# Grouped-query decode attention with a gated MLP: stretches of the TensorE program become loops, each head's closing work moves to the end of its group, and seven in place of five output slices go by 512-column matmuls

## The chip, the cores and the metric

The kernel runs on one core of a Trainium2 chip. The metric is device time in microseconds of that core, as a median of runs. All inputs lie in the chip's memory at the start, and the result is written there.

## The reference

Two tokens (B = 2) are decoded against a cache of 32,768 positions. Eight key/value heads serve 32 query heads, four queries a head, 128 elements each; everything is bf16.

```python
xn = _layernorm(x)
s  = _A_ref(xn, k_cache, v_cache, wq, wo)        # attention
g  = _silu(_B_ref(xn, w1, w2, w3, w4))           # MLP; with S = 1 its shifted halves are zero, so w1, w2 drop out
return x + s * g
...
q = (xn @ wq) per head;  scores = q.k * Dh**-0.5;  p = softmax(scores);  o = p.v;  s = o @ wo
h2 = gelu(layernorm(xn) @ w3) @ w4;  _B_ref = xn + h2
```

The two caches are 2 x 8 x 32,768 x 128 bf16 each, 134 MB; with `wq` (4 MB), `wo` (4 MB), `w3` and `w4` (1.8 MB each) 280.5 MB are read once.

## The kernel before, in words

**Groups.** A group is one (token, key/value head): 16 in all (`NG`). For each, K is one 8 MB DMA into two of the three slots of `kbuf`, V one 8 MB DMA into `vbuf`, which holds one group. All large DMAs are issued by SP, in one order: wq, w3, w4, K0, V0, K1, V1, and so on, then `wo` in six parts (`wo_parts`). K of group m waits on `pe.sem`, which TensorE raises when the first half of group m-1 is nearly scored (L702); V of group m waits on `ac.sem`, raised when ScalarE sees the values' product of group m-1 done (L495). The last group's K and V, and `wo`, come in smaller pieces.

**One group.** Counting groups from 0, a group runs thus. K's 128 rows a partition are two halves (`NPART`) of eight tiles (`NR`). VectorE transposes the 16 tiles (L589) into four buffers `T` (`T_BUFS`); TensorE takes them in pairs (`t_vt`) and multiplies each by `z`, the group's queries spread into a selection pattern, four 512-column matmuls a tile (L698), the first half into PSUM bank `sc[0]`, the second into `sc[1]`. VectorE waits for a tile's four matmuls before it overwrites that buffer (`used`). Then come maximum (`peak`, L568), a matmul that spreads it (`S`, L710), `shift`, Exp on ScalarE (L491), VectorE's transposes of the probabilities (L608), 64 matmuls with V in two halves (L722), and a matmul for the sums (L729). ScalarE copies the product `o` to `ob` (L496).

**A head's closing work** turns `ob` into a column of `oX`: `head_oT` on TensorE (four fp32 matmuls, L660), `head_on` on VectorE (sum, reciprocal and two products: L543 to L552, giving `on`), `head_xp` on TensorE (one matmul, L666), `head_out` on VectorE (L559, L565), a copy on GpSimd (L513). For group m this runs inside group m+1: `head_oT` between the two halves of the scores, `head_on` after tile 3 of the second half, `head_xp` after TensorE's tile 4 of the second half, `head_out` after the last transpose. So in group 0 it works on zeroed data. The last group's runs in `pe_output`.

**Ahead of the groups** stand layernorms, q (L403, 32 matmuls in four column blocks of the array, two transposes L408), `w3` (L424), gelu, `w4` (L439, 14 matmuls), sigmoid. V0 overwrites w3 and w4, so its issue waits for `w4`'s last matmul (`e_h2`, L454).

**Behind the groups** `pe_output` multiplies by `wo`. Slices k = 0 to 3 (part 0) come from `oX_w`, which a wide matmul (L740) and VectorE (`own_part`) make. A slice k < KC goes as four 512-column matmuls into `qrb` (L760); after the last of them ScalarE copies `qrb` to `wsum` (L646), and four fp32 matmuls with `comb` (L750) add it into `pro`. A slice k >= KC goes as 16 matmuls of 128 columns straight into `pro` (L768). KC is 5. VectorE then multiplies by the gate and adds x (L647, L648), and two small DMAs write the output.

TensorE's own program is one straight stretch ahead of the groups, one loop `pe_groups` over 16 groups, whose body is both halves unrolled, and `pe_output`.

Of the kernel before, what the change touches and what calls it, by code (L numbers as in the profile page):

```python
# [21 lines left out]
T_BUFS = 4  # L22
# [44 lines left out]
class LateQueue(Queue):  # L67
# [13 lines left out]

    def place(self):
        for emit, need, inc in self.kept:
            for s, v in need[:-1]:
# [34 lines left out]
def kernel(  # L119
# [37 lines left out]
    KC = 5  # L157
# [72 lines left out]
    sc = [bank(f"sc{i}") for i in range(NPART)]  # L230
# [49 lines left out]
    t_vt, t_vg, t_tv = (sem(f"t_{n}") for n in ("vt", "vg", "tv"))  # L280
# [26 lines left out]
    with tc.tile_critical(sync_engine=mybir.EngineType.Pool, no_gpsimd_drain=True):  # L307
# [20 lines left out]
        po.op(lambda e: e.memset(ob[:, :], 0.0), inc=(t_ob, 1))  # L328
# [5 lines left out]
        ve.op(lambda e: e.memset(S[:, 0:NPART * rep], 1.0), inc=(t_tv, 1))  # L334
# [55 lines left out]

        treg = qrb[:, :].bitcast(BF16)
# [6 lines left out]
        HH = Hq // NPART  # L398
        for i in range(NPART):
            for k in range(DK):  # L400
                for n in range(NQ):
                    last = k == DK - 1 and n == NQ - 1
                    e = pe.op(lambda t, i=i, k=k, n=n: t.matmul(  # L403
                        sc[i][32 * n:32 * n + B, :], lhsT=xT[:, k, :],
                        rhs=wq3[:, k, :].rearrange("p (h n y) -> p h n y", n=NQ, y=32)[:, i * HH:(i + 1) * HH, n, :],
                        start=(k == 0), stop=(k == DK - 1), tile_position=(0, 32 * n)),
                        e_xT, e_s00, inc=last)
            e = ve.op(lambda v, i=i: v.transpose(out=qT[:, i * 512:(i + 1) * 512], in_=sc[i][:, :]), e)  # L408
# [29 lines left out]
        for f in range(FK):  # L438
            e_h2 = pe.op(lambda t, f=f: t.matmul(  # L439
                h2[0:B, :], lhsT=h_bf[:, f * B:(f + 1) * B], rhs=w4v[:, f, :],  # L440
                start=(f == 0), stop=(f == FK - 1)), e, inc=f == FK - 1)
# [19 lines left out]
        for m in range(1, NG):  # L461
            base = m % 2
            if m < NG - 1:
                sp.op(lambda e, m=m, base=base: e.dma_start(
                    out=kbuf[:, base * SLOT:(base + NPART) * SLOT], in_=row_view(A_k_cache, *groups[m])),
                    (pe.sem, pe_0 + m), e_q, inc=(t_k[0], 16))
            else:
                for i, h in enumerate(order(m)):
                    sp.op(lambda e, m=m, h=h, base=base: e.dma_start(
                        out=kbuf[:, (base + h) * SLOT:(base + h + 1) * SLOT],  # L470
                        in_=row_view(A_k_cache, *groups[m])[:, h * SLOT:(h + 1) * SLOT]),
                        (pe.sem, pe_0 + m), inc=(t_k[i], 16))
            load_v(m, (ac.sem, ac_0 + m))
# [6 lines left out]

        def take(eng, s, n=1):
            eng.wait_ge(s, n).then_inc(s, -n)  # L482

# [46 lines left out]
        def used(par, n):  # L530
            return t_tv, par * N_T + n + 2 + (n >= NR) + (n >= NR + 5)
# [4 lines left out]
        def out_of(par, last=False):  # L536
            return t_tv, par * N_T + (2 if last else NR + 2)

        def turned(par, last=False):
            return t_tv, par * N_T + (3 if last else NR + 8)  # L540

        def head_on(c, par=0, last=False, behind=None):
            nc.vector.tensor_reduce(  # L543
                out=den[:, :], in_=S[:, 0:NPART * rep].rearrange("p (i h) -> p h i", h=rep),
                axis=AX.X, op=ALU.add).wait_op(*sum_of(par), "sem-ge").then_inc(*c.inc(t_d))
# [5 lines left out]
            nc.vector.wait_ge(*out_of(par, last))  # L551
            ins = nc.vector.tensor_mul(  # L552
                out=on[:, :, :], in0=oT[:, :].unsqueeze(1).broadcast_to([128, NQ, rep]), in1=recm[:, :, :]).wait_op(*e, "sem-ge")
            if last:
                ins.then_inc(t_vt, 1)
                behind()

        def head_out(c, par=0, last=False):
            nc.vector.tensor_mul(  # L559
                out=xm[:, :, :], in0=xp_b[:, :].rearrange("p (r h) -> p r h", r=NQ),  # L560
                in1=mask[:, :].unsqueeze(1).broadcast_to([128, NQ, rep])).wait_op(*turned(par, last), "sem-ge").then_inc(*c.inc(t_d))
# [64 lines left out]
        e_wd, e_ws, e_s = ((pe.sem, pe.n + NG + i) for i in (1, 2, 3))  # L626
# [12 lines left out]
        head_on(c, last=True, behind=own_part)  # L639
        e_oX[NG - 1] = head_out(c, last=True)  # L640
        for b in range(B):
            m, n = b * Hkv + KC, Hkv - KC - (b == B - 1)
            e_oXz = ve.op(lambda v, b=b, m=m, n=n: v.tensor_copy(
# [37 lines left out]
        pe.n, pe.seen = prologue.n + NG, prologue.seen  # L681
# [4 lines left out]
        for s, v in prologue._new((e_s00, e_const, e_hf, e_tf, e_s0)):  # L686
            nc.tensor.wait_ge(s, v)
        nc.br("pe_groups", engines=[PE])
        with nc.body("pe_groups", valid_engines=[PE]):
            for i in range(NPART):  # L690
                for r in range(NR):
                    if r % 2 == 0:
                        take(nc.tensor, t_vt, 2)
                    Tb = Ts[(i * NR + r) % T_BUFS][:, :].bitcast(BF16).rearrange("p (b c e) -> p b c e", b=NB, e=2)
                    zc = (NR - 1 - r) * rep
                    for nb in range(NB):
                        for w in range(2):
                            ins = nc.tensor.matmul(  # L698
                                sc[i][:, :], lhsT=z[:, nb, w, zc:zc + 128], rhs=Tb[:, nb, :, w],
                                start=(r == 0 and nb == 0 and w == 0),  # L700
                                stop=(r == NR - 1 and nb == NB - 1 and w == 1))
                            if i == 0 and r == NR - 1 and nb == 0 and w == 0:  # L702
# [30 lines left out]
            nc.regs_alu(turn, turn, 1, op=ALU.add)  # L733
            nc.br_lt(turn, NG, on_true="pe_groups", on_false="pe_output", engines=[PE])


        with nc.body("pe_output", valid_engines=[PE]):
            head_oT()
# [5 lines left out]
            take(nc.tensor, t_vt)  # L744
            head_xp()
            for i, (a, c, r0, r1) in enumerate(wo_parts):
                if i == 3:
# [5 lines left out]
                for k in range(a, c):  # L753
                    pe.wait(e_oXz if k >= KC else e_oX[(B - 1) * Hkv + k], (d_wo[i], n_wo[i]), *((e_wide,) if i == 0 else ()))
                    for r in range(r0, r1):
# [9 lines left out]
                        for n in range(NQ):  # L765
# [4 lines left out]
                                start=(i == 2 and r == r0 and n < OQ), stop=(last and n >= NQ - OQ), tile_position=(0, 32 * q)),  # L770
# [41 lines left out]
```

## Time and profile before

| | |
|---|---|
| median of 3 runs | 655.83 us (655.77 to 655.99) |
| span of the profiled execution, first to last instruction | 654.1 us |
| what lies around the span (median less span) | 1.7 us |
| bytes read | 280.50 MB |
| TensorE matmuls busy | 417.4 us (64%) |
| VectorE busy | 379.4 us (58%) |
| ScalarE busy | 39.7 us (6%) |
| GpSimd busy | 10.3 us (2%) |
| mean granted TensorE clock | 0.88 of full speed |

The timings and the profile are separate executions; the profile gives no total of its own beside the span, so the difference of 1.7 us is taken as the part outside it. Rows of the timeline read: start in us from the span's start, duration, engine, line, operation, tile written <- tiles read, count, and in brackets the idle time before it with what ended it. PE is TensorE, PEld its weight loads, DVE VectorE, ACT ScalarE, SP the queue that issues DMAs; a q behind an engine's name is its sequencer. Rows of the windows give, for a stretch of time, each engine's busy time, the granted TensorE clock, the DMA engines' mean busy share (over 1 where a packet is counted in the stretch in which it began) and GB/s.

### The profile page before, as it was taken

Reading aid. Unit: us, or ns where it says so; the run is one execution under the profiler, and the core shown is the slowest. Engines: PE = TensorE matmul, PEld = TensorE weight load, DVE = VectorE, ACT = ScalarE, POOL = GpSimd, SP = SyncE. Lnnn points to the kernel's source line nnn. Section 1 sums busy time; section 2 is a strip of 40 time slices with the busy share of each in tenths; the row PEclk is TensorE's granted clock in tenths of the full one; section 3 lists DMA queues with packets and bytes.
Section 4 is the critical chain, followed back from the end, with each engine's and each line's share of the span. In section 5 each row is a group of like instructions: output and inputs, shape, how many; then the busy total and the mean of one; then the engine's idle time right before and its main releaser. Section 6 shows DMA issues by size and latency. Waiting matters only on the chain. (4 is left out here: it accounts for less than half of the span.)

```text
span 654.1 us, 6304 instructions
## 1 busy us (share of the span) xinstructions
PE 417.4 (64%) x2476; PEld 159.3 (24%) x2476; DVE 379.4 (58%) x541; ACT 39.7 (6%) x90; POOL 10.3 (2%) x44
## 2 busy tenths in 40 slices
PE   1437386574858747485774838667484865748876
PEld 0013132221313212131321313222131322213223
DVE  5348193673919457291854729276481936738772
ACT  1200101000010100001000010100001010000101
POOL 1000000000000000000000000000000000000000
PEclk9859889697997969899796989969698896979999
DMA  8999999999999999998999999999999899999997
GB/s 367 435 449 449 442 393 449 445 449 401 437 445 449 433 405 449 445 449 389 449 445 449 417 421 445 449 445 393 449 445 449 389 449 445 449 425 411 437 429 292
DMA packets 6246, 280.54 MB, mean 429 GB/s; under 512 B 730, under 2 KB 868, under 8 KB 1380
## 3 DMA queue, kind: packets, MB, share of 16 engines
q1 hardware_dynamic: 6232, 280.50, 99.2%
q8 instruction: 2, 0.03, 0.0%
q10 hardware_dynamic: 12, 0.00, 0.0%
HBM read 280.50 MB, written 0.00 MB: 429 GB/s over the span
## 5 line engine op out<-in xcount | busy, mean ns | idle before, releaser
L589 DVE STREAM_TRANSPOSE T<-kbuf 128x1024 int32<-128x1024 int32 x256 | 294.8, 1211 | 180.1 <-DMA kbuf<-in_A_k_cache_dram 173.2
L698 PE MATMUL sc<-T,z 128*128 128x512 bf16 x1024 | 273.1, 420 | 179.5 <-PEq L482 179.2
L698 PEld LDWEIGHTS sc<-T,z 128*128 128x128 bf16 x1024 | 98.9, 104 | 346.6 <-issue 260.2
L722 PE MATMUL o<-vbuf,pt 128*16 128x512 bf16 x1024 | 70.4, 379 | 17.7 <-PEq L482 17.7
L491 ACT ACTIVATE ep<-sc,shift 128x512 bf16<-128x512 f32 x32 | 21.7, 683 | 502.7 <-ACTq L482 502.7
L722 PEld LDWEIGHTS o<-vbuf,pt 128*16 128x16 bf16 x1024 | 27.3, 88 | 64.9 <-issue 42.8
L568 DVE TENSOR_REDUCE mx<-sc 128x1 f32<-128x512 f32 x32 | 21.5, 672 | 30.1 <-PE sc L698 30.1
L673 PE MATMUL pro<-ob,comb 128*2 128x512 f32 x66 | 33.7, 592 | 0.0
L608 DVE STREAM_TRANSPOSE pt<-ep 128x512 bf16<-128x512 bf16 x32 | 22.6, 708 | 15.0 <-ACT ep L491 15.0
L710 PE MATMUL S<-mxr,same_h 128*128 128x448 f32 x32 | 15.8, 576 | 18.4 <-PEq L482 18.4
L660 PEld LDWEIGHTS oT<-sel_o,ob 128*128 128x128 f32 x136 | 17.7, 191 | 3.4 <-issue 0.7
L729 PE MATMUL S<-sm,ones_f 128*128 128x448 f32 x32 | 16.3, 592 | 0.0
L660 PE MATMUL oT<-sel_o,ob 128*128 128x4 f32 x136 | 16.2, 242 | 0.0
L600 DVE TENSOR_REDUCE shift<-S 128x1 f32<-128x64 f32 x16 | 3.6, 225 | 18.8 <-PE S L710 18.8
L496 ACT COPY ob<-o 128x512 f32<-128x512 f32 x16 | 9.4, 587 | 78.6 <-ACTq L482 78.6
L513 POOL COPY oX<-oXs 128x4 bf16 (+1 forms) x16 | 3.0, 188 | 518.7 <-POOLq L482 518.7
L710 PEld LDWEIGHTS S<-mxr,same_h 128*128 128x128 f32 x32 | 4.8, 188 | 26.1 <-issue 26.1
L572 DVE TENSOR_SCALAR mxr<-row_of,mx 128x32 f32<-128x32 f32 x32 | 7.7, 241 | 1.1
L673 PEld LDWEIGHTS pro<-ob,comb 128*2 128x2 f32 x66 | 4.2, 83 | 14.0 <-issue 10.4
L393 PE MATMUL qrb<-ident,xs_bf 34*128 34x34 bf16 x4 | 0.3, 198 | 11.1 <-DVE xs_bf L356 11.1
L729 PEld LDWEIGHTS S<-sm,ones_f 128*128 128x128 f32 x32 | 4.8, 188 | 6.9 <-issue 6.9
L506 POOL TENSOR_TENSOR z<-qr,quad 128x64 bf16<-128x64 bf16 x16 | 4.7, 294 | 103.2 <-POOLq L482 87.7
(100 smaller groups left out, 78.5 us busy)
## 6 DMA issues: line engine op xcount, KB each, us to landing
kbuf<-in_A_k_cache_dram SPq DMA_DIRECT2D x2, 4096.0 KB, 22.4
vbuf<-in_A_v_cache_dram SPq DMA_DIRECT2D x2, 4096.0 KB, 21.7
kbuf<-in_A_wq_dram SPq DMA_DIRECT2D x1, 4096.0 KB, 12.4
vbuf<-in_B_w_dram SPq DMA_DIRECT2D x2, 1792.0 KB, 18.0
kbuf<-in_A_wo_dram SPq DMA_DIRECT2D x1, 2048.0 KB, 30.8
kbuf<-in_A_wo_dram SPq DMA_DIRECT2D x3, 512.0 KB, 31.9
kbuf<-in_A_wo_dram SPq DMA_DIRECT2D x1, 384.0 KB
kbuf<-in_A_k_cache_dram SPq DMA_DIRECT2D x15, 27.5
```

Source lines behind the costliest of these rows:

```text
L491: nc.scalar.activation(out=ep[i][:, :], in_=sc[i][:, :], func=ACT.Exp, scale=inv_sqrt_dh, bias=shift[:, :], accum_out=rs[:, i:i + 1]).then ...
L496: nc.scalar.copy(out=ob[:, :], in_=o[:, :]).then_inc(t_ob, 1)
L568: ins = nc.vector.tensor_reduce(out=mx[:, i:i + 1], in_=sc[i][:, :], axis=AX.X, op=ALU.max)
L572: ins = nc.vector.tensor_scalar_mul(out=mxr[:, i, :], in0=row_of[:, :], scalar1=mx[:, i:i + 1]).wait_op(*c.at(t_d), "sem-ge")
L589: ins = nc.vector.transpose(out=Ts[n % T_BUFS][:, :].rearrange("p (b t k) -> p t b k", b=NB, t=RT), in_=kt[:, r * W:(r + 1) * W].rearrange ...
L608: ins = nc.vector.transpose(out=pt[h][:, :, :].rearrange("p r (t h) -> p t r h", h=rep), in_=ep[order(par).index(h)][:, :].rearrange("p (t ...
L660: ins = nc.tensor.matmul(oT[:, :], lhsT=ob[:, t * Dh:(t + 1) * Dh], rhs=sel_o[:, t, :], start=(t == 0), stop=(t == VT - 1))
L673: nc.tensor.matmul(pro[0:B, :], lhsT=comb[:, 0:B], rhs=ob[:, :], start=True, stop=True)
L698: ins = nc.tensor.matmul(sc[i][:, :], lhsT=z[:, nb, w, zc:zc + 128], rhs=Tb[:, nb, :, w], start=(r == 0 and nb == 0 and w == 0), stop=(r = ...
L710: nc.tensor.matmul(S[:, NPART * rep:NPART * (rep + SREP * 32)].rearrange("p (s c) -> p s c", s=SREP), lhsT=same_h[:, :], rhs=mxr[:, :, :]. ...
L722: ins = nc.tensor.matmul(o[32 * j:32 * j + VT * rep, :], lhsT=pt[h][:, r, a * VT * rep:(a + 1) * VT * rep], rhs=vt[:, u * VT:(u + 1) * VT, ...
L729: nc.tensor.matmul(S[:, 0:SSUM * NPART * rep].rearrange("p (s c) -> p s c", s=SSUM), lhsT=ones_f[:, :], rhs=sm[:, :, :].rearrange("p i h - ...
```

## The change

On TensorE:

- q is a loop of eight turns; each turn makes 512 columns by four matmuls into two PSUM rows (not four column blocks), alternating between the two banks, waits for `t_q`, and VectorE turns each chunk by four 32-partition transposes (32 in place of two).
- `w4`'s 14 matmuls are one, then a loop of six turns with two each, then one.
- The two halves of a group's scores are a loop of two turns over eight tiles; the bank is addressed by a register. `pe.sem` rises in both halves, and the counts of K's waits follow.
- `head_oT`, a wait for `on` (`t_on`) and `head_xp` stand at the end of the group's own body, ahead of the branch back; `pe_output` has no copies of them. TensorE takes `t_on` once before the first group too.
- The loop branches carry no branch hint; `pe_groups` had none before either.
- KC is 7, the comb matmuls stand ahead of the last part of `wo` (i == 5, not i == 3), and the single filler matmul `warm(1)` is gone.

On VectorE `head_on` stands after tile 2 of a group's first half, and `head_out` after tile 5. `oT` and `xp` are set to ones at the start. TensorE's program goes from 634 to 443 instructions.

```diff
+            if isinstance(emit, tuple):
+                nc, start, end, body = emit
...
+                with nc.Fori(start, end, engines=[PE]) as i:
+                    body(self.eng, i).then_inc(self.sem, 1)
...
-    KC = 5
+    KC = 7
...
-    sc = [bank(f"sc{i}") for i in range(NPART)]
+    sc2 = bank("sc", 512 * NPART)
+    sc = [sc2[:, 512 * i:512 * (i + 1)] for i in range(NPART)]
...
+        nc.vector.sem_inc(t_q, NPART)
...
+        def q_part(t, c):
+            take(t, t_q)
+            out_c = sc2[0:B, bass.ds((c & 1) * 512, 512)]
             for k in range(DK):
...
+                ins = t.matmul(
+                    out_c, lhsT=xT[:, k, :], rhs=wq3[:, k, bass.ds(c * 512, 512)],
+                    start=(k == 0), stop=(k == DK - 1))
+            return ins
+
+        pe.loop(nc, 0, NC, q_part, e_xT, e_s00)
+        for c in range(NC):
+            for n in range(NQ):
+                e = ve.op(lambda v, c=c, n=n: v.transpose(
...
+        def w4_part(t, j):
+            for i in range(W4N):
+                ins = t.matmul(
+                    h2[0:B, :], lhsT=h_bf[:, bass.ds(j * W4N * B + (1 + i) * B, B)],
+                    rhs=vbuf[:, bass.ds(j * W4N * D + W4O + (1 + i) * D, D)], start=False, stop=False)
+            return ins
...
+        pe.loop(nc, 0, (FK - 2) // W4N, w4_part)
...
-                    (pe.sem, pe_0 + m), e_q, inc=(t_k[0], 16))
+                    (pe.sem, pe_0 + NPART * (m - 1) + 1), e_q, inc=(t_k[0], 16))
...
+                        if i == 0 and r == 2:
+                            head_on(c, par)
+                        if i == 0 and r == 5:
+                            head_out(c, par)
                         if i == 1 and r == 3:
                             peak(c, 0)
-                            head_on(c, par)
-                head_out(c, par)
...
+        take(nc.tensor, t_on)
         nc.br("pe_groups", engines=[PE])
         with nc.body("pe_groups", valid_engines=[PE]):
-            for i in range(NPART):
+            with nc.Fori(0, NPART, engines=[PE]) as i:
...
-                                sc[i][:, :], lhsT=z[:, nb, w, zc:zc + 128], rhs=Tb[:, nb, :, w],
+                                sc2[:, bass.ds(i * 512, 512)], lhsT=z[:, nb, w, zc:zc + 128], rhs=Tb[:, nb, :, w],
...
-                    if i == 1 and r == 4:
-                        head_xp()
-                if i == 0:
-                    head_oT()
...
             nc.regs_alu(turn, turn, 1, op=ALU.add)
+            head_oT()
+            take(nc.tensor, t_on)
+            head_xp()
             nc.br_lt(turn, NG, on_true="pe_groups", on_false="pe_output", engines=[PE])
...
-            head_oT()
             pe.wait(e_sp, e_oX[NG - 2])
...
-            take(nc.tensor, t_vt)
-            head_xp()
             for i, (a, c, r0, r1) in enumerate(wo_parts):
-                if i == 3:
+                if i == 5:
...
-                    if i == 2:
-                        warm(1)
```

More of the change, by code (lines that the diff above doesn't have):

```diff
@@ L80, in op, with loop @@
         return None
+    def loop(self, nc, start, end, emit, *events):
+        self.kept.append(((nc, start, end, emit), self._new(events), True))
+        self.n += end - start
+        return (self.sem, self.n)
     def place(self):
         for emit, need, inc in self.kept:
+            if isinstance(emit, tuple):
+                nc, start, end, body = emit
+                for s, v in need:
+                    self.eng.wait_ge(s, v)
+                with nc.Fori(start, end, engines=[PE]) as i:
+                    body(self.eng, i).then_inc(self.sem, 1)
+                continue
             for s, v in need[:-1]:
@@ L278 @@
         n_wo[i] += 16
-    t_vt, t_vg, t_tv = (sem(f"t_{n}") for n in ("vt", "vg", "tv"))
+    t_vt, t_vg, t_tv, t_on, t_q = (sem(f"t_{n}") for n in ("vt", "vg", "tv", "on", "q"))
     t_z, t_ob, t_e, t_d, t_pv = (sem(f"t_{n}") for n in ("z", "ob", "e", "d", "pv"))
@@ L397 @@
             in_=treg[:, 0:64 * DK].rearrange("p (k s c) -> p s k c", k=DK, s=2)[:, :, :, 0:B]), e, (d_wq, 16))
-        HH = Hq // NPART
-        for i in range(NPART):
-            for k in range(DK):
[L401 to L408, printed above, removed]
+        HC = 512 // Dh
+        NC = Hq // HC
+        def q_part(t, c):
+            take(t, t_q)
+            out_c = sc2[0:B, bass.ds((c & 1) * 512, 512)]
+            for k in range(DK):
+                ins = t.matmul(
[6 more added lines that the diff above has]
+                e = ve.op(lambda v, c=c, n=n: v.transpose(
+                    out=qT[32 * n:32 * n + 32, c * 32 * HC:(c + 1) * 32 * HC],
+                    in_=sc[c % 2][0:32, :].rearrange("p (h n y) -> p n h y", n=NQ, y=32)[:, n, :, :]), (pe.sem, pe.n - NC + c + 1),
+                    inc=(t_q, 1) if n == NQ - 1 and c < NC - NPART else True)
         e_q = ve.op(lambda v: v.tensor_mul(
@@ L437 @@
         h2 = sc[1]
[L438 to L441, printed above, removed]
+        W4N = 2
+        def w4_part(t, j):
[4 more added lines that the diff above has]
+            return ins
+        assert (FK - 2) % W4N == 0
+        pe.op(lambda t: t.matmul(h2[0:B, :], lhsT=h_bf[:, 0:B], rhs=w4v[:, 0, :], start=True, stop=False), e, inc=False)
+        pe.loop(nc, 0, (FK - 2) // W4N, w4_part)
+        e_h2 = pe.op(lambda t: t.matmul(h2[0:B, :], lhsT=h_bf[:, (FK - 1) * B:FK * B], rhs=w4v[:, FK - 1, :], start=False, stop=True))
         e_tf = ve.op(lambda v: v.tensor_add(out=t_f[:, :], in0=xn[:, :], in1=h2[0:B, :]), e_h2)
@@ L638 @@
         e_wide = (ve.sem, ve.n + 2)
-        head_on(c, last=True, behind=own_part)
+        head_on(c, behind=own_part)
         e_oX[NG - 1] = head_out(c, last=True)
```

44 lines of the change are left out of this document (23 added, 21 removed).

## The prediction

> **What bounds the kernel now.** I read the page first, then the chain that ended last, then the DMA views, and only then the engines.
>
> ```profile
> span 654.1 us, 6304 instructions
> q1 hardware_dynamic: 6232, 280.50, 99.2%
> q8 instruction: 2, 0.03, 0.0%
> ```
>
> ```profile
> 617.12 33.53 DMA kbuf<-in_A_wo_dram
> ...
> 650.69 0.64 PE pro L768 x16
> ...
> 651.35 0.29 DVE sg L647
> ```
>
> The 16 DMA engines are busy 99.2% of the span with the 280.5 MB that must be read, and the chain ends in a DMA, 16 matmuls and two vector operations. So an edit to TensorE costs something only (1) if it makes SP issue a transfer so late that the DMA engines run dry, (2) if it lengthens the work behind the last landing, or (3) if it changes the DMA stream itself. For (1) I need the slack of each issue:
>
> ```profile
> DMA packets 5225, 249.40 MB, mean 433 GB/s; under 512 B 583, under 2 KB 601, under 8 KB 1097
> ...
> kbuf<-in_A_wq_dram SPq DMA_DIRECT2D x1, 4096.0 KB, 12.4
> ...
> DMA to landing us min/median/max: 26.0/26.7/33.0
> ...
> DMA to landing us min/median/max: 26.6/27.5/28.7
> ...
> DVE T L589 <- DMA kbuf<-in_A_k_cache_dram: 173.2, 17, 12.7
> ```
>
> At 433 GB/s (DMA view of 72.8 to 649 us) 8.39 MB take 19.4 us. The first DMA, which had no queue ahead, landed 12.4 us after its issue, 9.7 of them transfer: 2.7 us are fixed. A V (first of the two landing rows, L448) took at least 26.0, so it stood 26.0 - 19.4 - 2.7 = 3.9 us in the queue; a K (second, L464) 4.5 us; V0, the 33.0, 10.9 us. VectorE waits 173 us in all for K, some 10 us a group: compute inside a group is hidden as long as an issue moves by less than those slacks.
>
> **The change part by part.**
>
> *Ahead of the groups: covered.*
>
> ```profile
> 13.51 3.26 PE L403 MATMUL sc<-kbuf,xT 128*2 128x512 bf16 x32 [2.07 <-DVE xT L395]
> ...
> 16.83 0.72 DVE L408 STREAM_TRANSPOSE T<-sc 128x512 f32<-128x512 f32 x1 [0.68 <-PE sc L403]
> ...
> 24.23 3.18 PE L439 MATMUL sc<-vbuf,h_bf 128*2 128x512 bf16 x14 [2.38 <-DVE h_bf L436]
> 27.45 0.36 SPq L448 DMA_DIRECT2D vbuf<-in_A_v_cache_dram  x1
> ```
>
> q takes 13.51 to 17.55 with four column blocks side by side. One after the other, as L439 does the same shape (3.18 / 14 = 0.227 each), 32 take 7.3. A loop turn's waits, register operations and branch are shown by no row of q; bounds 0 (the sequencer ahead of the array) and 0.5 us; I take 0.3, near the branch row below, for eight turns 2.4. Four transposes of the last chunk: a quarter of 0.72 each at least, 0.22 with a start, 0.9 together. Sum 10.6 for 4.04: +6.5; `w4`'s six turns +0 to +1.5, taken +0.5. V0 is issued near 34.5, inside its slack of 10.9; even +9 for q is. If the cover were gone, the excess would be lost one for one. K0's compute waits for K0 in any case.
>
> *Inside a group: hidden, except in the last two.* I follow group 14, whose delay is handed to group 15, which the end follows.
>
> ```profile
> 583.11 5.75 DVE L589 STREAM_TRANSPOSE T<-kbuf 128x1024 int32<-128x1024 int32 x5 [10.97 <-DMA kbuf<-in_A_k_cache_dram]
> ...
> 585.62 9.32 PE L698 MATMUL sc<-T,z 128*128 128x512 bf16 x32 [8.66 <-PEq L482]
> ...
> 589.23 8.10 DVE L589 STREAM_TRANSPOSE T<-kbuf 128x1024 int32<-128x1024 int32 x7 [0.38 <-PE sc L698]
> ...
> 598.10 0.16 DVE L543 TENSOR_REDUCE den<-S 128x4 f32<-128x8 f32 x1
> ...
> 598.80 4.61 DVE L589 STREAM_TRANSPOSE T<-kbuf 128x1024 int32<-128x1024 int32 x4
> ...
> 603.34 0.13 DVE L559 TENSOR_TENSOR xm<-xp,mask 128x16 f32<-128x16 f32 x1
> 603.51 0.17 DVE L565 TENSOR_REDUCE oXs<-xm 128x4 bf16<-128x16 f32 x1
> ...
> 605.56 0.69 DVE L568 TENSOR_REDUCE mx<-sc 128x1 f32<-128x512 f32 x1 [1.88 <-PE sc L698]
> ...
> 612.08 9.13 DVE L589 STREAM_TRANSPOSE T<-kbuf 128x1024 int32<-128x1024 int32 x8 [1.76 <-DMA kbuf<-in_A_k_cache_dram]
> ...
> 614.12 1.02 PE L729 MATMUL S<-sm,ones_f 128*128 128x448 f32 x2
> ...
> 621.88 4.62 DVE L589 STREAM_TRANSPOSE T<-kbuf 128x1024 int32<-128x1024 int32 x4 [0.67 <-DMA kbuf<-in_A_k_cache_dram]
> ```
>
> ```profile
> 586.40:589.80 3.40, 3.40 (x9) 1.17 (x8) 3.02 (x4) 0.00 (x0) 0.00 (x0) 0.51 0.89 386
> ```
>
> ```profile
> L734 PEldq COMPARE_BRANCH x16: 76/208/228, 70.6 to 641.8; - x16
> ```
>
> TensorE now starts a group after two transposes. Changed, it stands at `t_on`, behind three transposes (583.11 + 3.45) and `head_on` (598.10 to 598.80, 0.70, and 0.1 for its end), with `head_xp`, the branch back (0.21 by the last row) and the loop's entry branch (another 0.21) behind that; with 0.3 for xp, waits and registers, 0.7. Scores start at 588.05, not 585.62: +2.4, a new wait, and what is queued behind it is the whole group's scores, for which VectorE's buffers wait. The clock is at 0.5 there (nine matmuls in 3.40 us), so tile 0's four matmuls end at 589.9 and tile 1's at 591.6. VectorE, back from `head_on`, has its buffers full at 588.4: it waits 1.5 for tile 0 and 0.55 for tile 1, against 0.38 now. `head_out` costs it 0.35 in the middle, where it was hidden in the 1.88 wait at 605.56. `head_on` only moves, `head_oT` falls into TensorE's idle time. Group 14's VectorE work, and so V's issue and the product with V, comes 2.05 - 0.38 + 0.35 = 2.0 us later, K's issue 2.4. Both are inside 3.9 and 4.5: no bubble, 2 us left.
>
> Group 15's K is there when group 14 ends, so this case differs: `on` is ready 2.33 us after the start of the sums' matmul (643.29 to 645.62 in the rows of the end), 614.12 + 2.0 + 2.33 = 618.45. Until then VectorE stands behind `head_on` after three tiles, where now it runs eight without a stop. TensorE starts at 619.15, tile 0 is through at 620.15 with a warm clock, VectorE's tiles 4 to 7 and `head_out` end at 625.0. The second half begins 3.1 later than 621.88, gets 0.70 back since `head_on` is no longer in it: everything behind it +2.4.
>
> *Behind the groups.*
>
> ```profile
> 643.29 1.02 PE L729 MATMUL S<-sm,ones_f 128*128 128x448 f32 x2
> ...
> 645.20 0.22 PE L740 MATMUL sc<-T,sel_w 128*128 128x128 bf16 x1
> ...
> 645.45 0.17 DVE L552 TENSOR_TENSOR on<-oT,recm 128x16 bf16<-128x16 f32 x1 [0.52 <-PE oT L660]
> ...
> 646.41 1.04 PE L760 MATMUL qrb<-kbuf,T 128*2 128x512 bf16 x16
> ...
> 647.29 0.39 PE L760 MATMUL qrb<-kbuf,oX 128*2 128x512 bf16 x4
> 647.74 0.59 ACT L646 COPY T<-qrb 128x512 f32<-128x512 f32 x1 [3.57 <-PE qrb L760]
> ...
> 649.07 0.81 PE L750 MATMUL pro<-T,comb 128*4 128x128 f32 x8
> ```
>
> The path is now compute to 647.3 and landings to 650.69. Changed: `on` 2.33 after L729's start; xp, the branch not taken (0.08) and the wide matmul's issue 0.4; wide matmul to part 0 as now (645.20 to 646.41) 1.2; part 0's 16 matmuls 0.9; twelve for k = 4, 5, 6 at 0.054 each (16 in 0.87), 0.65; their end 0.23; copy of `qrb` with its hand-over 0.65; comb 0.65 (under the modelled 0.81); the last four and their end 0.25. Together 7.26 from L729, which starts at 643.29 + 2.4: 652.95. Part 3's landing no longer ends last, the copy and comb do. Against 651.35 that is **+1.6**. The single operations are rows; the hand-overs may be off by 0.1 each, so +1.0 to +2.2.
>
> *The DMA stream.*
>
> ```profile
> q8 instruction: 1, 0.02, 5.2%
> ```
>
> ```profile
> 650.00:650.50 0.50, 0.36 (x14) 0.17 (x7) 0.00 (x0) 0.00 (x0) 0.00 (x0) 1.00 0.05 20
> ```
>
> Two packets of the whole run are instructions. One lies in 71.7 to 72.8 us (first row): 5.2% of 16 engines times 1.1 us is 0.92 us on one engine, which all the others do not lose; the view of 72.8 to 649 has none (its 5225 packets are all of q1). The other comes past 648.5. At the very end (second row) the mean share is 0.05, under one engine of 16: one engine still moves `wo` when the others are done, and TensorE waits for it. An engine that fetched 16 KB in group 0 is late by 0.92 in every later transfer. If the shorter program needs no such fetch while the groups stream, K14, K15 and `wo` all land up to 0.9 earlier: **-0.9** (bounds 0 and -0.92), on the compute chain as well, since it starts at K14. I take it, because at the time of the packet TensorE was in the last 140 of the 445 instructions that end its group loop, and the changed loop ends at its 328th.
>
> [...]
>
> [...]
>
> Sum against the profile: 654.1 + 1.6 - 0.9 = 654.8; the 1.7 us outside the span stay: **656.5** beside the median of 655.83.
>
> **The rivals.**
>
> [...]
>
> *The stream runs dry.* V's issue has 2 us left. Should the groups start later than I have it by more than 2 us (the cold stretch longer, the loop's addressing slow), each group loses the excess: 0.5 us too much is 15 x 0.5, 664. It decides from a V issue 3.9 us later than now. Against: every price in that path has a row.
>
> *Taken branches fetch.* Each turn's branch back could need its code again: a packet of 0.92 behind one of V's. Two a group would use up the 2 us left and lose about 1 us in each of 16 groups, and 14 turns of 0.92 ahead of V0 exceed its remaining 3.9 by 9: some 656 + 16 + 9 = 681. Against: the row has 15 taken branches over 305 instructions and one packet. [...]
>
> *The end stays hidden.* If my hand-overs at the end are too dear and the landings still end last, only the fetch counts: 655.83 - 0.9 = 654.9. For it: five slices' worth of matmuls shrink. Against: VectorE standing still behind `head_on` in group 15 is in the program's order.
>
> **How the numbers follow.** Forecast 0.48 (656.5, +-0.7), fetch stays 0.32, dry 0.05, branches fetch 0.03, hidden end 0.12. About 0.2%, 1.3 us, is what a measurement here can tell from no change: above 657.1 or below 654.5. Slower: two thirds of the second case, the third and fourth, and a tenth of the forecast, 0.35. Faster: a third of the last and a little of the forecast, 0.05. The range from 655.0 to 658.0 leaves out part of the last case, the dry and fetching ones and a sliver of the second.
>
> **What would show it.** V0 issued near 34.5; V's landing rows no lower than 23.9; scores starting 4.9 us, not 2.5, after a group's first transpose; VectorE idle 1.5 us for TensorE at tile 4; in group 15 VectorE waiting on the sums; the end's chain through the copy of `qrb` and comb; no instruction packet between 0 and 640 us. Wrong would be: landings at 99% but a shorter time than 654.5, K or V issued after the queue is empty, or a chain that still ends in `wo`'s DMA.

## The result, and the profile after

| | before | after |
|---|---|---|
| median | 655.91 us (655.77 to 656.47), in the same session | 662.68 us (662.01 to 662.82), 4 runs |
| ratio to before, 95% interval | | 1.010 (1.0086 to 1.0114) |
| span of the profiled execution | 654.1 us | 658.0 us |
| time of the profiled execution, and what of it lies around the span | 1.7 us by the median | 662.76 us, 4.8 us |

The changed kernel is slower by 6.8 us, and the time lies outside the predicted range. I read the same views as before, in the same order. First the page:

```profile
span 658.0 us, 6506 instructions
...
q1 hardware_dynamic: 6232, 280.50, 98.8%
q8 instruction: 1, 0.02, 0.0%
```

The span is only 3.9 us longer. The other 3 us or so of the loss lie outside it, where the prediction had put nothing. The same 6232 packets now fill 98.8% instead of 99.2%. One 16 KB instruction packet is left of two; the one that is gone is the one near the end (649.5 us before). Next, the chain that ended last, in order of time (start, duration, what):

```profile
650.72 0.17 PE xp L701
...
652.17 1.64 PE qrb L792 x28
...
653.83 0.59 ACT T L681
...
654.47 0.61 PE pro L782 x8
...
655.23 0.29 DVE sg L682
```

`wo`'s DMA is gone from it: the end is now 28 wide matmuls, ScalarE's copy of `qrb` and the comb matmuls, as predicted. `sg`, the product with the gate behind the last matmul, starts at 655.23, 3.88 us later than before (651.35).

**Ahead of the groups.** The timeline of after, from q to V0's issue:

```profile
16.03 1.32 DVE L431 STREAM_TRANSPOSE T<-sc 32x128 f32<-32x128 f32 x4 [2.67 <-PE sc L423]
...
20.63 2.68 DVE L431 STREAM_TRANSPOSE T<-sc 32x128 f32<-32x128 f32 x8 [0.23 <-PE sc L423]
...
26.43 1.32 DVE L431 STREAM_TRANSPOSE T<-sc 32x128 f32<-32x128 f32 x4 [0.21 <-PE sc L423]
27.79 0.58 DVE L435 TENSOR_TENSOR q_sb<-T,cls 128x256 bf16<-128x256 f32 x1
...
34.56 0.38 PE L474 MATMUL sc<-vbuf,h_bf 128*2 128x512 bf16 x1 [2.39 <-DVE h_bf L462]
34.91 4.62 PE L468 MATMUL sc<-vbuf,h_bf 128*2 x12
...
39.79 0.36 SPq L483 DMA_DIRECT2D vbuf<-in_A_v_cache_dram  x1
```

A chunk's four small transposes take 1.3 us, so VectorE works almost without a pause from 16.03 to 27.75 (four waits for TensorE, 1.0 us together) and sets the length of q. `w4` takes 5.2 us up to V0's issue (34.56 to 39.79) where it took 3.2 (24.23 to 27.45). V0 is issued 12.3 us later than before. What that does to the DMA queue stands in the landings of V (L483):

```profile
DMA to landing us min/median/max: 22.0/24.6/25.5
```

V0 is the minimum, 22.0 us. The working of the prediction had 19.4 us of transfer plus 2.7 fixed for a DMA with no queue ahead of it, which is 22.1: V0 met an empty queue. Everything behind it stays late. Group 14's first transpose, which starts when its K has landed ("K14" below), comes at 584.34 instead of 583.11, 1.2 us later:

```profile
584.34 3.50 DVE L620 STREAM_TRANSPOSE T<-kbuf 128x1024 int32<-128x1024 int32 x3 [9.51 <-DMA kbuf<-in_A_k_cache_dram]
...
589.40 9.97 PE L734 MATMUL sc<-T,z 128*128 128x512 bf16 x31 [0.57 <-PEq L407]
591.33 1.25 DVE L620 STREAM_TRANSPOSE T<-kbuf 128x1024 int32<-128x1024 int32 x1 [1.66 <-PE sc L734]
...
617.71 1.02 PE L761 MATMUL S<-sm,ones_f 128*128 128x448 f32 x2
...
618.77 0.17 DVE L574 TENSOR_REDUCE den<-S 128x4 f32<-128x8 f32 x1 [1.32 <-PE S L761]
...
619.87 0.17 DVE L583 TENSOR_TENSOR on<-oT,recm 128x16 bf16<-128x16 f32 x1 [0.51 <-PE oT L695]
...
620.98 9.00 PE L734 MATMUL sc<-T,z 128*128 128x512 bf16 x31 [0.62 <-PEq L407]
...
648.24 1.02 PE L761 MATMUL S<-sm,ones_f 128*128 128x448 f32 x2
```

**In the groups.** These are the last two groups in the timeline. The scores start 5.06 us after the first transpose (589.40 less 584.34; 2.5 before), VectorE then stands 1.66 us for tile 0, and in group 15 it stands for the sums of group 14. The sums' matmuls start at 617.71 and 648.24 instead of 614.12 and 643.29: +3.59 and +4.95, of which 1.23 came with K14.

**The clock** in the windows of after over group 15's first half; the third number from the right is the granted clock:

```profile
618.00:622.00 4.00, 2.95 (x16) 1.57 (x16) 1.84 (x5) 0.59 (x1) 0.00 (x0) 1.00 0.95 410
622.00:626.00 4.00, 4.00 (x13) 1.41 (x11) 3.48 (x5) 0.00 (x0) 0.19 (x1) 0.57 0.97 418
```

From 622 to 626 TensorE was granted 0.57 of its speed. The same windows of before:

```profile
618.00:622.00 4.00, 3.43 (x15) 1.19 (x14) 3.33 (x4) 0.00 (x0) 0.00 (x0) 1.00 0.91 393
622.00:626.00 4.00, 3.71 (x22) 2.13 (x20) 4.00 (x4) 0.00 (x0) 0.00 (x0) 1.00 0.93 401
```

There the clock is full in both, and VectorE is busy for 3.33 of the first 4 us, where it is for 1.84 in after. Group 14 has a low stretch in every run, over its start: it ends at 589.8 before (6.7 us after K14) and at 594.9 in after (10.6 us after K14). In a_prol, a version with before's q and `w4` that is taken up below, it ends 7.9 us after K14. Windows of after and of a_prol some 8 us behind their K14:

```profile
592.00:596.00 4.00, 4.00 (x13) 1.46 (x12) 3.31 (x6) 0.00 (x0) 0.19 (x1) 0.64 1.17 508
```

```profile
591.00:595.00 4.00, 4.00 (x19) 1.68 (x17) 3.83 (x6) 0.00 (x0) 0.19 (x1) 0.97 1.17 508
```

**Behind the span.** The DMA view of after from 658.5 to 664 us, past the last instruction of the span:

```profile
q14 instruction: 1, 0.01, 0.3%
```

An 8 KB packet of instructions is fetched at 660.9 us. The profile of before has no packet past its span. And in the DMA view of after from 74 to 77 us, in group 0, the packet that the prediction had taken away is still there:

```profile
q8 instruction: 1, 0.02, 1.9%
```

So the 6.9 us between the two profiled executions split into three: 3.1 outside the span (1.7 to 4.8), 1.2 in the DMA stream, and 2.65 of compute from K14's first transpose to `sg` (70.89 us, 655.23 less 584.34, against 68.24). Each got experiments of its own.

### The profile page after: what moved, and what is told of

It reads as the page before. It is cut to its first block, busy times and chain, and to the rows that moved or that the text cites. A ratio compares the mean times of both kernels' runs of the same rounds, so it can differ in the third digit from the quotient of the medians.

```text
span 658.0 us, 6506 instructions
## 1 busy us (share of the span) xinstructions
PE 435.0 (66%) x2410; PEld 161.8 (25%) x2442; DVE 389.9 (59%) x572; ACT 39.7 (6%) x90; POOL 10.3 (2%) x44
## 3 DMA queue, kind: packets, MB, share of 16 engines
q1 hardware_dynamic: 6232, 280.50, 98.8%
## 5 line engine op out<-in xcount | busy, mean ns | idle before, releaser
L620 DVE STREAM_TRANSPOSE T<-kbuf 128x1024 int32<-128x1024 int32 x256 | 299.5, 1217 | 164.4 <-DMA kbuf<-in_A_k_cache_dram 131.2
L701 PE MATMUL xp<-on,sel_w 128*128 128x16 bf16 x16 | 2.7, 171 | 110.7 <-PEq L407 110.7
L701 PEld LDWEIGHTS xp<-on,sel_w 128*128 128x128 bf16 x16 | 1.7, 104 | 111.6 <-issue 111.6
L695 PEld LDWEIGHTS oT<-sel_o,ob 128*128 128x128 f32 x128 | 15.5, 191 | 11.1 <-issue 11.1
L761 PE MATMUL S<-sm,ones_f 128*128 128x448 f32 x32 | 16.3, 592 | 0.0
L423 PE MATMUL sc<-kbuf,xT 128*2 x32 | 9.8, 442 | 5.0 <-PEq L407 4.1
L431 DVE STREAM_TRANSPOSE T<-sc 32x128 f32<-32x128 f32 x32 | 9.8, 307 | 4.6 <-PE sc L423 3.7
## 6 DMA issues: line engine op xcount, KB each, us to landing
vbuf<-in_A_v_cache_dram SPq DMA_DIRECT2D x2, 4096.0 KB, 19.4
kbuf<-in_A_wq_dram SPq DMA_DIRECT2D x1, 4096.0 KB, 12.3
```

The lines of the kernel that those rows point to most:

```text
L423: ins = t.matmul(out_c, lhsT=xT[:, k, :], rhs=wq3[:, k, bass.ds(c * 512, 512)], start=(k == 0), stop=(k == DK - 1))
L431: e = ve.op(lambda v, c=c, n=n: v.transpose(out=qT[32 * n:32 * n + 32, c * 32 * HC:(c + 1) * 32 * HC], in_=sc[c % 2][0:32, :].rearrange("p ...
L620: ins = nc.vector.transpose(out=Ts[n % T_BUFS][:, :].rearrange("p (b t k) -> p t b k", b=NB, t=RT), in_=kt[:, r * W:(r + 1) * W].rearrange ...
L695: ins = nc.tensor.matmul(oT[:, :], lhsT=ob[:, t * Dh:(t + 1) * Dh], rhs=sel_o[:, t, :], start=(t == 0), stop=(t == VT - 1))
L761: nc.tensor.matmul(S[:, 0:SSUM * NPART * rep].rearrange("p (s c) -> p s c", s=SSUM), lhsT=ones_f[:, :], rhs=sm[:, :, :].rearrange("p i h - ...
```

## The experiments

Names beginning with `a` stand for versions of the kernel after, with `b` for versions of the kernel before. All ratios are to runs of the kernel before on the same chip.

| run | median, us | ratio (95%) | outside the span, us | V0 issued at | group 14's first transpose |
|---|---|---|---|---|---|
| after | 662.68 | 1.010 (1.0086 to 1.0114) | 4.5 to 4.8 | 39.79 | 584.34 |
| a_prol | 658.88 | 1.0038 (1.0024 to 1.0052) | 1.8 | 29.44 | 583.42 |
| a_pad | 662.96 | 1.0097 (1.0080 to 1.0114) | 4.5 | 40.31 | 585.40 |
| b_prol | 659.83 | 1.0059 (1.0042 to 1.0076) | 4.4 to 4.5 | 39.73 | 584.27 |
| b_w4 | 656.11 | 1.0002 (0.9992 to 1.0011) | 1.8 | 29.42 | 583.38 |
| b_q32 | 658.69 | 1.0046 (1.0031 to 1.0060) | 4.4 to 4.5 | 36.96 | 583.45 |
| b_dve | 656.37 | 1.0007 (0.9997 to 1.0016) | 2.3 to 2.4 | 29.21 | 583.05 |
| b_dve32 | 658.69 | 1.0045 (1.0028 to 1.0062) | 4.4 to 4.7 | 29.53 | 582.98 |
| b_dve64 | 656.19 | 1.0005 (0.9995 to 1.0014) | 1.8 | 29.36 | 583.46 |
| b_kc7 | 656.71 | 1.0011 (1.0001 to 1.0021) | 1.9 | 29.40 | 583.29 |
| b_loop | 658.93 | 1.0042 (1.0028 to 1.0056) | 1.8 | 27.76 | 583.35 |
| a_late | 656.58 | 1.0012 (1.0002 to 1.0022) | 1.8 | 27.83 | 583.25 |
| a_all | 658.17 | 1.0029 (1.0017 to 1.0042) | 1.8 | 40.53 | 585.38 |

"Outside the span" is a run's time less its span; the last two columns are of the profiled execution. V0's issue near 29.4 does not mark a changed prologue: a_prol, b_kc7 and the three b_dve have `w4` written out as before. In them a stretch of half clock lies over `w4`, whose 14 matmuls then take 4.8 to 4.9 us instead of 3.18.

### The change cut at the start of the groups: a_prol and b_prol

a_prol is after with q and `w4` written out as in before; b_prol is before with only those two loops.

```diff
-        pe.loop(nc, 0, NC, q_part, e_xT, e_s00)
...
+                for n in range(NQ):
+                    last = k == DK - 1 and n == NQ - 1
+                    e = pe.op(lambda t, i=i, k=k, n=n: t.matmul(
+                        sc[i][32 * n:32 * n + B, :], lhsT=xT[:, k, :],
...
-        pe.loop(nc, 0, (FK - 2) // W4N, w4_part)
...
+        for f in range(FK):
+            e_h2 = pe.op(lambda t, f=f: t.matmul(
```

> The changed kernel with q and w4 unrolled as before (everything else changed). Theory 1: the loops ahead of the groups issue V0 at 39.8 us and let the DMA engines run dry for 1.3 us; here V0 goes out near 27.5, the first K after it lands at 80.9 as before, and the span falls from 658.0 to about 656.7, the rest (closing work at the end, 2.6 us) staying. Rival: V0's lateness is covered by what is queued and the loss comes from the groups themselves: span 657.5 to 658.1. The part outside the span: 4.7 us if it goes by where TensorE's program ends (507 instructions, against 450 in the change and 637 before); 1.7 us if it was a matter of the loops ahead of the groups.

> The kernel before with q and w4 as loops (580 instructions). Theory 1: V0 at 39.8, the engines dry for about 1.3 us, everything behind it later by that: span 655.4 to 655.6 instead of 654.1. Rival (covered): 654.1. [...]

The two are complementary and add up: +2.7 us without the prologue's loops, +3.6 with them alone (each against before in the same session), 6.3 together against 6.8 for the whole change. The prologue's 3.6 us are not only the DMA stream: b_prol's span is 655.3, 1.2 us over before, and the rest lies outside it, with the packet behind the end at 658.1 us. So what these loops bring ahead of the groups costs some 2.7 us after the last instruction, 600 us later.

### Is it TensorE's program? a_pad

After with 96 tiny matmuls ahead of the groups, so that TensorE's program is as long as before (642 instructions against 637; this count has 450 for after, where the description of the change has 443).

```diff
+        for _ in range(96):
+            nc.tensor.matmul(o[0:2, 0:4], lhsT=ident[:, 0:2], rhs=ident[:, 0:4], start=True, stop=True)
         take(nc.tensor, t_on)
         nc.br("pe_groups", engines=[PE])
```

> The changed kernel with 96 tiny matmuls (192 instructions) added on TensorE ahead of the groups, where it stands idle for K0: TensorE's program is as long as before (642 against 637). [...]

The time stays at after's (662.96), 4.5 us are outside the span, and the packet behind the end is there, at 661.7. The number of TensorE's instructions decides neither.

### The w4 loop alone, and q in the new form without a loop: b_w4 and b_q32

b_q32's edit of before, in part:

```diff
-        HH = Hq // NPART
-        for i in range(NPART):
+        HC = 512 // Dh
+        NC = Hq // HC
+
+        def q_part(t, c, k):
...
+        for c in range(NC):
             for k in range(DK):
...
+                pe.op(lambda t, c=c, k=k: q_part(t, c, k), e_xT, e_s00, inc=k == DK - 1)
```

> The kernel before with only w4 as a loop of six turns. Theory 1: two matmuls and a turn take 0.79 us instead of 0.45, V0 is issued about 2 us later (29.5 to 31.5), far inside its slack: span 654.4, outside 1.8, time 656.2, no change. Rival (TensorE loops ahead of the groups cost the part outside): outside 4.4 and time 658.9.

> The kernel before with q computed in the change's form, 8 chunks of 4 matmuls and 32 small transposes on VectorE, but written out in TensorE's program, without a register loop (w4 is unrolled as before too). Theory A: 4.4 us outside the span and a packet behind the end as with the loop; theory B: 1.8 us outside. For the length of the stage both expect that the transposes decide it: 32 of 0.31 us are 9.9 us where the loop's stage had 13.7, so q ends 4-6 us before the loop's does if the turns (waits, branch) cost anything, or within 1.5 us of it if VectorE alone sets it; V0's issue then is 33-38 us instead of 27.5 without and 39.8 with both loops, under the 37.5-38.5 at which the DMA engines ran dry, so that the span stays at 654-654.6.

The `w4` loop moves V0 by 2 us and costs no time. Its price is not the clock's: b_w4's loop took 5.2 us at full clock, where before's 14 matmuls took 3.2. Written out under the half clock they need nearly as long, as in b_kc7. Windows over `w4` in b_w4 and in b_kc7:

```profile
24.20:29.40 5.20, 4.08 (x14) 1.08 (x14) 0.00 (x0) 0.71 (x1) 0.00 (x0) 1.00 0.93 403
```

```profile
24.50:29.40 4.90, 4.80 (x14) 1.39 (x14) 0.02 (x1) 0.82 (x1) 0.00 (x0) 0.66 0.99 428
```

b_q32, without any TensorE loop, has the 4.4 us outside and the packet behind the end: the loop is not the cause, what VectorE does for q is. Its q is also nearly as long as the loop's, as its timeline shows:

```profile
18.98 8.09 DVE L430 STREAM_TRANSPOSE T<-sc 32x128 f32<-32x128 f32 x24 [0.39 <-PE sc L421]
...
36.96 0.36 SPq L473 DMA_DIRECT2D vbuf<-in_A_v_cache_dram  x1
```

24 transposes in 8.09 us, 0.34 each, without a pause: they end at 27.07, only 0.7 us ahead of after's 27.75. So the transposes set the stage and TensorE's turns hide behind them nearly whole. With V0 at 36.96 the span is 654.5 and group 14 starts at 583.45, as in the runs with V0 near 29 (583.0 to 583.5); with 39.73 (b_prol) it starts at 584.27. The point at which the engines run dry lies between, where the prediction's slack of 10.9 puts it (27.45 + 10.9 = 38.35).

### How long is VectorE's program? b_dve, b_dve32, b_dve64

Before, with 30, 32 and 64 one-column memsets in VectorE's program ahead of the groups:

```diff
         e_s0 = ve.op(lambda v: v.memset(pro[:, :], 0.0))
+        for _ in range(32):
+            nc.vector.memset(more[:, _:_ + 1], 0.0)
```

VectorE's program has 158 instructions before, 190 after, 189 in b_prol and b_q32, and 188, 190 and 222 in these three.

> The kernel before with 30 one-column memsets added to VectorE's program ahead of the groups, where it waits for K0; nothing else. In the runs so far the part outside the span is 1.8 us where q is unrolled (before, a_prol, b_kc7) and 4.4 to 4.8 where it is a loop with 32 small transposes (the change, a_pad, b_prol), whatever TensorE's length, and an 8 KB instruction packet lies behind the end in those alone. Theory 1 (second form): it is VectorE's program, 30 instructions longer, whose code behind the kernel then has to be fetched when all else is done: span 654.4 as before, outside 4.4 to 4.8, time near 658.9. Rival: it is TensorE's loops ahead of the groups: outside 1.8, time 656.2.

> The kernel before with 32 one-column memsets more in VectorE's program, ahead of its groups: VectorE's program then has 190 instructions as the changed kernel's (158 before; 189 with the prologue's loops in before; 188 with 30 memsets). Theory A (VectorE's program has grown over a border of what is fetched ahead, so that what runs behind the kernel's last instruction is fetched late): the part of the time outside the profiled span goes from 1.8 to 4.4-4.7 us, an 8 KB instruction packet shows up behind the last instruction, the span stays at 654.1, and the time is 658.5-659. Theory B (TensorE's register loop over q is the cause): the part outside stays at 1.8 to 2.4 us and the time is 656.0-656.6.

> The same with 64 memsets more (222 instructions for VectorE). The 30 memsets tried first had 2.35 us outside the span instead of 1.8, without a packet behind the end. Theory A: 4.4-5 us outside, a packet behind the end, time 658.5-659.5 (the prologue is some 3 us longer on VectorE and stays inside the slack of the first V load). Theory B: no packet behind the end, 1.8 to 2.4 us outside, 656.0-656.8.

30 memsets moved nearly nothing (0.5 us outside the span), and alone would have acquitted VectorE. Two more cost 2.3 us: b_dve32's span is that of before, 654.0, and the loss is all outside. Its DMA view from 654.5 to 660 us:

```profile
q14 instruction: 1, 0.01, 0.4%
```

With 64 the loss is gone. That is the number that theory B had given for this run, but b_dve32 and b_q32, which lose without a TensorE loop, rule B out; A needs another form. The page of b_dve64 counts its packets within the span:

```profile
q8 instruction: 2, 0.03, 0.0%
q14 instruction: 2, 0.02, 0.0%
```

Now two 8 KB packets come in the run (at 28.3 and 188.6 us) and none behind it. So it is not how much VectorE does, but where its program ends. With 188 instructions or fewer no 8 KB packet comes after the start; with 189 or 190 one comes behind the last instruction, and the run pays 2.6 to 2.9 us; with 222 two come during the run, none behind it, and 1.8 us lie outside the span, as in before. That the code run behind the kernel's last instruction comes with the late packet is my reading of this order; no row names what was fetched. Nor does every packet behind the end cost time: a_late, below, has a 16 KB one of queue q8 at 656.1, past its span of 655.8, and still only 1.8 us outside. Its DMA view from 655.8 to 658.5 us:

```profile
q8 instruction: 1, 0.02, 2.2%
```

### KC 7 alone, and the groups' new order: b_kc7, b_loop, a_late

b_kc7 is before with KC 7, comb one part later and no filler. b_loop is before with the scores' loop and the closing work at the group's end (KC 5, prologue as before). a_late is a_prol with the loop kept, but with `t_on` and `head_xp` behind the scores and `head_on` behind tile 3 of the second half, as in before:

```diff
-                        if i == 0 and r == 2:
-                            head_on(c, par)
-                        if i == 0 and r == 5:
-                            head_out(c, par)
                         if i == 1 and r == 3:
                             peak(c, 0)
+                            head_on(c, par)
                 peak(c, 1, *used(par, NT - 1))
+                head_out(c, par)
...
+            take(nc.tensor, t_on)
+            head_xp()
             take(nc.tensor, t_vt)
...
             head_oT()
-            take(nc.tensor, t_on)
-            head_xp()
```

> The kernel before with KC = 7, comb ahead of the last part, without warm (587 instructions). Span: k = 6 lands at 649.7, then 0.4 for its matmuls, 0.65 for the copy, 0.65 for comb, 0.25 for the last four: 651.6 against 651.35, span 654.2 to 654.5. A rival says 16 matmuls a slice less shorten the end: 653.9. [...]

> The kernel before with the scores' loop and the closing work at the group's end alone (q and w4 unrolled, KC 5). Theory 1: nearly all of a_prol's 2.7 us are here, since KC = 7 alone cost 0.5: span 656.5 to 656.9, outside 1.8, time 658.3 to 658.8. Rival: the loss in a_prol comes from KC = 7 meeting a later chain: 656.8 to 657.3 in time.

> a_prol (q and w4 unrolled, scores' loop, KC 7) with the wait for on and head_xp behind the scores' loop, head_on back behind tile 3 of the second half and head_out behind the last maximum; head_oT stays at the group's end. Theory 1: what costs at the end is that in group 15 TensorE's scores and VectorE's transposes stand for on; without that stand the second half begins near K15's second landing as before, and the span is 654.9 to 655.5 (0.5 of it KC 7) against a_prol's 657.1; scores start 2.5 us after a group's first transpose. Rival: the loop over the halves itself (branches, addressing) is what costs: span 656.5 or more.

KC 7 alone costs 0.5 us, little more than the noise (95%: 0.1 to 1.4). The loop over the scores' chunks is free: a_late, which keeps it, stands with b_kc7, 0.6 and 0.5 us over before. The new order with its wait for `on` ahead of the scores costs the rest: a_prol is 2.7 over before, 2.1 more than a_late. b_loop, with KC 5, loses 2.9 us by that order alone, so the two prices do not add up: under the new order KC 7 shows no price of its own. In a_prol's timeline the sums of group 15 start at 646.02, 62.6 us after K14, against 60.2 before: +2.4.

```profile
583.42 3.50 DVE L602 STREAM_TRANSPOSE T<-kbuf 128x1024 int32<-128x1024 int32 x3 [9.38 <-DMA kbuf<-in_A_k_cache_dram]
...
616.18 1.02 PE L743 MATMUL S<-sm,ones_f 128*128 128x448 f32 x2
...
646.02 1.02 PE L743 MATMUL S<-sm,ones_f 128*128 128x448 f32 x2
```

In a_late's they start at 643.43, 60.2 us after K14 (583.25):

```profile
612.22 4.62 DVE L602 STREAM_TRANSPOSE T<-kbuf 128x1024 int32<-128x1024 int32 x4 [1.72 <-DMA kbuf<-in_A_k_cache_dram]
614.31 1.02 PE L742 MATMUL S<-sm,ones_f 128*128 128x448 f32 x2
...
616.44 5.36 PE L713 MATMUL sc<-T,z 128*128 128x512 bf16 x23
...
643.43 1.02 PE L742 MATMUL S<-sm,ones_f 128*128 128x448 f32 x2
```

VectorE fills all four buffers while TensorE still works on group 14, and it does not wait for that group's sums.

### Two of the three costs repaired, the loops kept: a_all

After with 34 memsets more on VectorE (223 instructions) and a_late's order; all loops, KC 7 and the late V0 stay.

> The changed kernel with all its loops over q, w4 and the scores' chunks and with KC 7, but (1) 34 one-column memsets more in VectorE's program (223 instructions instead of 190), and (2) the output projection's waits late again as in a_late (head_on and head_xp behind the second half's tiles, the wait for on behind the scores' loop). Theory (the three costs found are separate: 2.7 us behind the end by the length of VectorE's program, 2.3 us by the wait for on ahead of the scores, 1.0 us by the late V0): 662.7 - 2.7 - 2.3 = 657.7, that is a_late's 656.6 plus the 1.0 us of the dry engines; the part outside the span is 1.8, no packet behind the end, V0's issue at 40, and group 14's first transpose at 584.3. Rival (the loops cost more in the groups than was seen, a bubble behind K2 or a slower turn): 659 or above with the part outside at 1.8. Rival (the length of VectorE's program does not explain the changed kernel's own 4.5 us): the part outside stays at 4.4 to 4.7 and the time is 660.4.

658.17: the two rivals fall, nothing is left outside the span but 1.8 us, and 4.5 of after's 6.8 us are gone. It is 0.5 above the sum expected. In the profiled execution, a slower one (658.71), K14 comes 1.1 later than expected; V0 went out at 40.53, 0.7 later than in after, and there is no slack left to take that up. An 8 KB packet now comes at 23.4 us, in the middle of q, but it is not shown to be the reason: VectorE's eight transposes around it take 2.68 us, as in after, and a_pad, without such a packet, has V0 at 40.31 and K14 at 585.40. Most of the delay arises in the `w4` loop (34.73 to 40.53, 5.8 us against 5.2). Why K14 moves by more than V0 stays open. No version here beat before.

## Why the prediction was wrong

The profiled execution of after took 662.76, 6.3 us over the forecast. By its own steps:

**"the 1.7 us outside the span stay"** is the largest miss, +3.1 us. It was treated as a constant. With 32 instructions more on VectorE an instruction packet comes behind the last instruction and 4.4 to 4.7 us lie outside the span (b_dve32), with 64 none comes there and it is 1.8 (b_dve64); these two change nothing else. In the changed kernel it is shown by a_all (223 instructions, 1.8). The prediction counted instructions on TensorE alone and listed the 30 transposes more only by their duration.

**"V0 is issued near 34.5, inside its slack of 10.9"** failed by its size. The slack was right. The sum took 6.5 us for q and 0.5 for `w4`; they took 10.2 (`q_sb` starts at 27.79, 17.59 before) and 2.0. The step that failed within it is that TensorE's 32 matmuls set q's length, with only the last chunk's transposes behind them. A small transpose was priced at a quarter of the big one's 0.72 with a start, 0.22; it takes 0.31, and 32 of them are 9.8 us: VectorE became the bound of the stage, and b_q32 shows it. The price of a `w4` turn was bounded at 1.5 us for six turns; it was 2.0. "Even +9 for q is" inside the slack would have held for q alone, but not for q's 10.2 with `w4`'s 2.0. V0 at 39.79 is 1.4 past the slack, and the stream lost 1.2.

**"-0.9", the fetch leaves group 0,** did not happen: the packet is there at 75.4 in after (71.7 before), at 71.7 to 78.5 in every version, whether TensorE's program had 450 or 642 instructions (as counted for a_pad). That a shorter program does without it was an assumption of mine that no run shows; the case that the fetch stays, to which the prediction gave 0.32, held on this point. That its going would have brought 0.9 us was therefore not tested. With the 1.2 us of the dry engines the stream term is +1.2 instead of -0.9, 2.1 us off.

**"+2.4" in the groups and "+1.6" at the end.** The mechanism was right: TensorE stands at `t_on`; V and K stay inside their slack; VectorE waits 1.66 us at tile 4 (predicted 1.5) and, in group 15, 1.32 us for the sums. a_prol's +2.4 is the predicted number, in part by luck: its groups 14 and 15 lost 1.75 and 0.68, where the working had 2.0 and 0.4. In after itself they lost 2.36 and 1.36, together 3.7 (4.95 less 1.23), and the tail from L761 to `sg` took 6.99 (predicted 7.26), so +2.65 instead of +1.6. The term that was mis-sized is the clock. The working took it as low for tiles 0 and 1 of group 14 only, and as full in group 15 ("tile 0 is through at 620.15 with a warm clock"). The missing 1.3 is the difference between after and a_prol, 0.6 in group 14 and 0.7 in group 15. In after the low stretch of group 14 lasts 2.7 us longer behind K14 than in a_prol, and group 15 has one of 3.4 us from 622.2 that a_prol has not. a_pad, whose two stretches lie as in after's, lost the same: 33.37 us from K14 to the sums of group 14 in both, and 30.5 from there to those of group 15 (a_prol: 32.76 and 29.85). That the clock is the cause is argued from these traces; no run changed the clock alone. In a_prol the same kind of stretch falls into the tail instead, as its windows show, and the tail takes 8.6 us:

```profile
618.00:626.00 8.00, 6.41 (x29) 2.61 (x30) 6.78 (x9) 0.00 (x0) 0.19 (x1) 1.00 1.02 442
649.00:653.00 4.00, 4.00 (x35) 1.13 (x36) 0.99 (x5) 0.00 (x0) 0.00 (x0) 0.57 0.25 93
```

What sets off such a stretch was not tried.

**Sum of the misses:** 3.1 + 2.1 + 1.3 - 0.3 (tail) = 6.2, of 6.3. The rival "the stream runs dry" named the right event at the wrong place: V0 alone, once, not a bubble in each group. "Taken branches fetch" is refuted: the turns of the loops ahead of the groups and a branch back more in each group brought no packet (one of instructions in after's span, two in before's). "The end stays hidden" fell as well, since the chain no longer ends in `wo`'s DMA; what it had for it, five slices that shrink, are two (KC 5 to 7).

## What to carry to other kernels

Fold a loop on one engine only after counting what it adds on the others, in time and in instructions: here the shorter TensorE program made VectorE's longer, and both of its prices, 10 us of small transposes and a fetch behind the end, were outside TensorE. When time is lost outside the span, look for an instruction packet behind the last instruction, and move the end of each engine's program by a few dozen cheap instructions before blaming any work (here 32 memsets gave 4.4 to 4.7 us outside, 64 gave 1.8); one packet there (a_late) cost nothing. The wait that was put ahead of a group's first matmul was hidden behind the DMA in the early groups (a_prol's group 14 starts 0.3 us later than before's) and paid at the end (2.4 us in a_prol), where the last group's data is already there.

## What was not expected of the hardware

- The end of the program cost 2.6 to 2.9 us here that no instruction shows. Two memsets (b_dve to b_dve32) turned it on, 32 more turned it off; at 188 instructions 0.5 us of it showed, without a packet, which stays unexplained.
- A 32x128 fp32 transpose out of PSUM takes 0.31 us in after (L431, 32 of them), while one of 128x512, sixteen times as large, takes 0.72 in before (L408).
- Six turns of two register-addressed matmuls cost 0.33 us a turn more than the same matmuls written out (2.0 us over six, at full clock in b_w4 and before). Whether the branch or the addressing costs it was not separated.
- The granted TensorE clock falls to half again and again. In before and in after each group but the last has a stretch over its start, mostly 10.2 us long, that begins while TensorE stands idle for K (group 14 of before: 579.5 to 589.8, with TensorE idle from 577.0 to 585.6). Shorter ones of 3.4 us come near the end of the run, and not in the same place: at 622 in after, at 649 in a_prol, at both places in b_loop's profiled run, which is that kernel's longest (661.06 against a median of 658.93). Its windows:

```profile
619.00:623.00 4.00, 3.15 (x9) 1.20 (x10) 2.17 (x2) 0.00 (x0) 0.00 (x0) 0.61 1.03 442
650.00:654.00 4.00, 3.85 (x27) 1.71 (x28) 1.07 (x6) 0.00 (x0) 0.00 (x0) 0.57 0.03 9
```
